# Loads as streams of their own, exchanges on two queues and a new order of requests in a gated mix of a long convolution and a dilated window attention

## The chip, the core and the metric

The kernel runs on one core of a Trainium2 chip. The core has five engines with instruction queues of their own: TensorE (PE, matrix products), VectorE (DVE), ScalarE (ACT), GpSimd (POOL) and SyncE (SP), which here does nothing but issue transfers. Transfers issued by SP go through the transfer queue that the profile calls q1, those of POOL through q0, and the few of ACT through q10; all three are served by the same 16 DMA engines of the core. The metric is device time in microseconds (us), lower is better. Three runs of the kernel before gave 229.2, 229.69 and 222.53 us, median 229.2.

## The reference, cut to what matters

```python
# x = A_q, k, v: [1, 2048, 640] bf16; shift_k: [640, 4]; ssm_k: [640, 2048]; ssm_D: [640]; wqkv: [640, 1920]; wo: [640, 640]
def A(q, k, v):                                   # H3-like branch
    k_shift = causal convolution of k over the sequence with 4 taps per channel (shift_k)
    kv = k_shift * v
    y = irfft(rfft(pad(kv)) * rfft(pad(ssm_k)))[:2048]      # causal convolution of length 2048, per channel
    return q * (y + kv * ssm_D)
def B(x):                                         # attention branch, 32 heads of 20 features
    q, k, v = split(x @ wqkv)
    logits = q[s] . k[s - 2w] for w = 0..7, times 20 ** -0.5, masked below 0
    return softmax(logits) @ v[s - 2w], heads joined, @ wo
g = sigmoid((x * gate_w).sum(-1))
out = g * A(x, k, v) + (1 - g) * B(x)
```

## The kernel before, in words

**Attention.** The rows of x are loaded into `xn` in eight pieces of 256 rows, transposed on PE (L445) into `xT`, even and odd positions apart, so that the dilation of two becomes a plain window. v is projected in 36 units of five matmuls (L521), and the gate in 20 (L534). q and k are projected (L568) for five feature tiles of 128 features (`ft` 0 to 4); one tile needs 12 units of five matmuls, six for q and then six for k (in the first tile they alternate). A unit's result is copied to a staging tile `stg`. Since a head has 20 features and the scores need every head at a partition that is a multiple of 32, the rows of each head are moved from `stg` by transfers of up to 20 rows, the **exchanges** (L618, `fragger`), into three sets of tiles `kb`, `qb`, which in the orders below carry the numbers 80/81, 82/83 and 84/85. A set holds four heads, one **head group**; the eight groups take the three sets in turn. For each group PE computes scores in five score groups (L642), ACT exponentiates each in two halves (L650, `ETall<-PS`), PE multiplies with v (L674) and DVE normalises (L684, L686).

**Convolution.** The four taps run on DVE in eight chunks (L467 to L482), the product with v behind them (L486). The long convolution is a transform in two steps: step one (L705 for the filter h, L701 for the signal u), step two (L724, with the table G), each for two halves P = 0, 1 of the channels; results are copied out of PSUM by ACT (L243) or DVE (L245). For the filter a copy `Hw` with swapped partitions is made by the **swaps** (L820): per half four pairs of transfers of 320 KB each, and from the second pair of a half on a one-column copy on POOL (L814) makes each pair wait until the pair before has landed. The **products** of the two spectra (L756) run on DVE, in 11 steps per half with two instructions each; the first needs the half's whole `Hw`. Then follow the inverse step one (L835), and the last step (L912), whose output `yb` is multiplied by the gated q (L890 scales q by g, L924 multiplies), added to the attention result `bl` (L926) and stored (L929). The output projection of the attention branch (L869) fills PE in between; its result is scaled into `bl` by ACT (L874) or DVE (L876).

**What sets the order.** Every part is a Python generator that yields requests (`Req`): which engine it wants, what it depends on, how many of four PSUM slots it takes. A string of some 1,100 letters, `ORDER`, says which stream is served next, and a `-` ahead of a letter gives the request to the second of two engines that it allows (ACT or DVE for a copy). The instructions of each engine stand in the order in which the requests were served, and each engine runs its own in that order. A request that waits therefore holds up everything behind it on its engine; on SP this is every later load and exchange. In the kernel before, the first loads are written out in `heads()`, in a fixed order; all later loads hang on the exchanges, through `bulk(ft)`, which `fragger` runs after the exchanges of a feature tile. Seven of the exchanges (q of the first feature tile) are issued by SP, the other 65 by POOL. `paced` loads have a small POOL memset ahead of the transfer.

## Time and profile before

| | us |
|---|---|
| three runs | 229.2, 229.69, 222.53 |
| median of them | 229.2 |
| profiled execution, its own time | 224.23 |
| its span | 222.5 |
| busy in the span: PE, DVE, ACT, POOL | 204.3, 185.0, 174.9, 51.1 |

The span is the time from the first to the last event that the profile shows; the profiled execution took 1.7 us more than its span. Three of the five engines are busy for 79% to 92% of the span, so no engine alone sets the time, and the busy figure of PE counts matmuls whose ends are modelled. The page is therefore read by stages: a table of windows gives each engine's busy time within a stretch, the chain of waits says what ended last at each place, the timelines give the start of single instructions, and the groups by line and shape the mean duration of one. In a timeline the second number is how long a piece lasted; instructions of one engine overlap a little, so the distance of two starts is less than the duration.

### The profile page before, as it was taken

How to read it: one execution, taken by the hardware profiler on the slowest of the kernel's cores; microseconds unless marked ns; L12 is line 12 of the kernel's file. 1: busy time of each engine (PE TensorE's matmuls, PEld its weight loads, DVE VectorE, ACT ScalarE, POOL GpSimd, SP SyncE). 2: the span in 40 equal slices, each digit the busy share in tenths (PEclk: the TensorE clock that was granted, in tenths of full speed). 3: DMA queues.
4: the chain of work that ended last, by engine and by line, in shares of the span. 5: the costliest groups of instructions: out<-in, count | busy, mean ns of one | idle time of the engine just before them, and what ended most of it. 6: DMA issues, size and time to landing. Idle time of an engine off the chain costs nothing.

```text
span 222.5 us, 8401 instructions
## 1 busy us (share of the span) xinstructions
PE 204.3 (92%) x3577; PEld 165.8 (75%) x3577; DVE 185.0 (83%) x261; ACT 174.9 (79%) x253; POOL 51.1 (23%) x129
## 2 busy tenths in 40 slices
PE   7999999999999999699997867999999999979990
PEld 3777987696777577466685756889888899979880
DVE  4745778997998898569898978998999997859992
ACT  0264487769998898599999988998999999478770
POOL 7980711470617044402450000000000000000000
PEclk9999999999999999999999699999999999999999
DMA  6999789599999999803993396678567082003645
GB/s 199 349 237 275 188 180 205 133 168 149 208 182 197 163 151 155 140 4 52 183 171 74 85 214 152 172 174 213 122 142 227 4 184 55 3 3 91 152 106 136
DMA packets 69049, 33.35 MB, mean 150 GB/s; under 512 B 51476, under 2 KB 66708, under 8 KB 69012
## 3 DMA queue, kind: packets, MB, share of 16 engines
q1 hardware_dynamic: 65684, 27.66, 61.3%
q0 software_dynamic: 2880, 4.90, 9.9%
q8 instruction: 28, 0.46, 1.0%
q10 hardware_dynamic: 448, 0.26, 0.4%
q14 instruction: 9, 0.07, 0.1%
HBM read 19.51 MB, written 2.62 MB: 100 GB/s over the span
## 4 chain that ended last, share of the span: by engine, by line
PE 51%; DVE 20%; ACT 10%; DMA 8%; issue 7%; POOL 2%; DVEq 0%; POOLq 0%; ACTq 0%
PE PS L568 14%; PE PS L521 8%; ACT ETall L650 6%; PE PS L835 6%; DMA kb<-stg 6%; DVE UC L245 5%; PE PS L869 4%; PE PS L724 4%; PE PS L674 3%; DVE SX L245 3%; PE PS L642 3%; DVE q L926 2%; DVE yb L245 2%; ACT H L243 2%; DVE q L924 2%
## 5 line engine op out<-in xcount | busy, mean ns | idle before, releaser
L650 ACT ACTIVATE ETall<-PS 121x912 bf16<-121x912 f32 (+1 forms) x80 | 63.8, 864 | 8.1 <-PE PS L642 7.7
L568 PE MATMUL PS<-xT,Wqk 128*128 128x342 bf16 (+1 forms) x300 | 49.7, 310 | 0.6 <-ACT stg L243 0.3
L243 ACT CAST UC<-PS 128x1024 bf16<-128x1024 f32 (+2 forms) x49 | 44.4, 1030 | 4.0 <-DVE UC L245 3.1
L568 PEld LDWEIGHTS <-Wqk 128*128 128x128 bf16 x300 | 27.4, 97 | 14.3 <-issue 0.5
L521 PE MATMUL PS<-WvT,xT 128*121 128x320 bf16 x180 | 27.5, 300 | 0.1
L467 DVE TENSOR_TENSOR KX<-KX 128x1280 bf16<-128x1280 bf16 x32 | 25.3, 820 | 0.3
L618 POOL DMA_DIRECT2D qb<-stg x29 | 14.6, 506 | 45.8 <-ACT stg L243 30.5
L869 PE MATMUL PS<-wo,oT 128*128 128x320 bf16 x160 | 24.4, 302 | 0.1
L521 PEld LDWEIGHTS <-xT 128*121 128x121 bf16 x180 | 23.4, 134 | 1.4
L243 ACT CAST stg<-PS 128x363 bf16<-128x363 f32 (+1 forms) x39 | 17.1, 471 | 7.8 <-PE PS L568 7.5
L869 PEld LDWEIGHTS <-oT 128*128 128x128 bf16 x160 | 21.1, 145 | 1.5 <-issue 0.5
L724 PEld LDWEIGHTS <-G 64*128 64x128 bf16 x512 | 18.2, 93 | 4.9 <-issue 3.7
L618 POOL DMA_DIRECT2D kb<-stg x36 | 18.1, 511 | 15.8 <-ACT stg L243 7.6
L642 PE MATMUL PS<-qb,kb 31*128 31x114 bf16 x576 | 16.0, 212 | 5.1 <-DMA kb<-stg 2.3
L245 DVE CAST stg<-PS 128x342 bf16<-128x342 f32 (+1 forms) x21 | 11.0, 522 | 11.7 <-PE PS L568 9.4
L642 PEld LDWEIGHTS <-kb 31*128 31x128 bf16 x576 | 9.4, 93 | 13.5 <-issue 9.8
L674 PEld LDWEIGHTS <-ETall 121*128 121x128 bf16 x576 | 17.4, 96 | 2.1 <-issue 0.5
L674 PE MATMUL PS<-VW,ETall 121*128 121x63 bf16 (+2 forms) x576 | 18.2, 184 | 0.6 <-DVE SX L245 0.3
L835 PE MATMUL PS<-F,Hw 128*128 128x128 bf16 x160 | 18.1, 219 | 0.0
L874 ACT ACTIVATE bl<-PS,omg 128x320 bf16<-128x320 f32 x31 | 16.1, 566 | 2.4 <-PE PS L869 1.9
L835 PEld LDWEIGHTS <-Hw 128*128 128x128 bf16 x160 | 17.9, 114 | 0.0
L245 DVE CAST UC<-PS 128x1024 bf16<-128x1024 f32 x13 | 15.3, 1219 | 2.6 <-ACT UC L243 1.2
(75 smaller groups left out, 334.1 us busy)
## 6 DMA issues: line engine op xcount, KB each, us to landing
xn<-in_A_q_dram SPq DMA_DIRECT2D x8, 320.0 KB
h_lin<-in_A_ssm_k_dram SPq DMA_DIRECT2D x16, 160.0 KB
vin<-in_A_v_dram SPq DMA_DIRECT2D x8, 320.0 KB
Hw<-H SPq DMA_DIRECT2D x8, 320.0 KB
q<-in_A_q_dram SPq DMA_DIRECT2D x8, 320.0 KB
Hw<-SX SPq DMA_DIRECT2D x8, 320.0 KB
kb<-stg POOLq DMA_DIRECT2D x28, 85.1 KB, 5.5
out_dram<-q SPq DMA_DIRECT2D x16, 120.0 KB
```

The costliest lines, as they stand in the source:

```text
L243: nc.scalar.copy(dst, src)
L245: nc.vector.tensor_copy(dst, src)
L467: eng.tensor_tensor(d, kin[:, n + 3 - j:n + 3 - j + m, :], w.to_broadcast([128, m, QC]), ALU.mult)
L521: nc.tensor.matmul(ps[0:BK, 0:320], lhsT=xT[:, dt, s0:s0 + BK], rhs=Wv[:, dt, 320 * hp:320 * hp + 320], start=(dt == 0), stop=(dt == NDT - 1))
L568: nc.tensor.matmul(ps[:, 0:n], lhsT=Wqk[:, dt, w, 128 * ft:128 * ft + 128], rhs=xT[:, dt, s0:s0 + n], start=(dt == 0), stop=(dt == NDT - 1))
L618: (nc.sync if near else nc.gpsimd).dma_start(dst[r0:r0 + rows, 0:wd], stg[fa - f0:fb - f0, 0:wd])
L642: nc.tensor.matmul(psum(g, h4 // 2)[:, h4 % 2, BQ * bb:BQ * bb + BQ], lhsT=kb[r:r + DH + NF, BK * b:BK * b + 128], rhs=qb[r:r + DH + NF, B ...
L650: nc.scalar.activation(ETall[0:BK, e, :, 0:BQ * nb], psum(g, k)[0:BK, :, 0:BQ * nb], ACT.Exp, scale=SCALE)
L674: nc.tensor.matmul(O[:, (b - b0) // 6, c0:c0 + 21 * nh], lhsT=ETall[0:BK, e, hh, BQ * bb:BQ * bb + 128], rhs=VW[0:BK, b, 4 * t + h4:4 * t ...
L724: nc.tensor.matmul(ps[:, c, 160 * jj:160 * jj + 160], lhsT=G[rows, j0 + jj, 64 - 64 * rr:192 - 64 * rr], rhs=Am[rows, rr].rearrange("p o ( ...
L835: nc.tensor.matmul(d, lhsT=st[(key, P)][:, c, o + il // 4, :, il % 4], rhs=M[:, k, :], start=(k == 0), stop=(k == 1), skip_group_check=True)
L869: nc.tensor.matmul(op, lhsT=oT[:, ft].rearrange("p h m a -> p a (h m)")[:, t, :], rhs=wo[:, ft, 320 * n:320 * n + 320], start=(ft == 0), s ...
```

## The change

- The loads of x, of the weights (`load_w0`, `load_w1`, `load_wv`), of k, of h, of the table G and of v become eight kinds of streams of their own, each with a letter in `ORDER`, and are no longer tied to the exchanges of a feature tile. k is loaded in six pieces of rows and not three; the first four of them have no POOL memset ahead. The tap weights `wraw` are issued by ACT and not by SP.
- Every exchange but those of q in the first feature tile may go to POOL or SP, as `ORDER` says. 39 now stand on SP (7 before) and 33 on POOL (65 before).
- The products take six steps per half and not 11: five of two steps each (1,920 columns per instruction, 960 before) and a last one of 640 columns. Each half has 12 product instructions, and not 22.
- `ORDER` is new as a whole, and with it the order on every engine. The constants that changed beside it (`LAND`, `STARTS`, `PIPE0`, `us`, `move`, costs) are estimates for the tool that made `ORDER`; they put out no instruction.

```diff
-KROWS = [(42, 64), (20, 42), (0, 20)]
+KROWS = [(53, 64), (45, 53), (37, 45), (29, 37), (13, 29), (0, 13)]
+FIRST = 4
...
 ORDER = """
-a-aa-aw-wa-aw-ww-wiiai-iiaaiaa-aia-iii-aiaa-ii-iiii-ii-iiiicifffccccw-wwww-wwwwfwwwwf-wffffwwwwwwcwcccccwwwdw-wdwddddi-wfccccccii
+ap-apquppqpptaaa4-a6-66666iia-aia-aa-attt-iiitti-iraii-aaai-iri-iivfu-iitiiiiii5tcff6fi-cc-ccc66fffff6666c-cc6666666666-66-66666cc
...
+    def load_x():
+        for a in range(2, 8):
+            yield from load(f"x{a}", xn[:, a], raw(x2, 256 * a * D, [[2 * D, 128], [D, 2], [1, D]]), 1150.0)
+
+    def load_w0():
+        for w in range(2):
+            yield from load(f"W0{w}", Wqk[:, :, w, 0:128], W3[:, :, w, 0:128], 800.0)
...
-            yield from paced(f"k{k}{q}", kin[32 * q:32 * q + 32, 3 + n0:3 + n1, :], raw(k2, n0 * D + QC * q, [[64 * D, 32], [D, n1 - n0], [1, QC]]), 62.0 * (n1 - n0))
+            yield from (paced if k >= FIRST else load)(f"k{k}{q}", kin[32 * q:32 * q + 32, 3 + n0:3 + n1, :], raw(k2, n0 * D + QC * q, [[64 * D, 32], [D, n1 - n0], [1, QC]]), 48.0 * (n1 - n0))
...
-    def bulk(ft):
-        if ft == 0:
-            yield from load_k(1)
-            yield from load_k(2)
-            yield from load_corners()
-            yield from small()
-            yield from load_h(0)
-        if ft == 1:
-            for a in range(4):
-                yield from load_G(a)
-                yield from load_v(0, a)
...
+    def load_ks():
+        for k in range(len(KROWS)):
+            yield from load_k(k)
+        yield from load_corners()
+
+    def load_h0():
+        yield from small()
+        yield from load_h(0)
+
+    def load_Gs():
+        for a in range(4):
+            yield from load_G(a)
+
+    def load_vs(c):
+        for a in range(4):
+            yield from load_v(c, a)
+
+    def load_h1():
+        yield from load_h(1)
...
+        for q in range(4):
+            nc.scalar.dma_start(wraw[32 * q:32 * q + 32].rearrange("p c j -> p (c j)"), raw(A_shift_k, 4 * QC * q, [[0, 32], [1, 4 * QC]]))
...
-                    g = yield Req("G", 510.0, deps, move=28.0 * rows)
-                (nc.sync if near else nc.gpsimd).dma_start(dst[r0:r0 + rows, 0:wd], stg[fa - f0:fb - f0, 0:wd])
+                    g = yield Req("GS", dict(G=510.0, S=450.0), deps, move=28.0 * rows)
+                (nc.sync if g.eng == "S" else nc.gpsimd).dma_start(dst[r0:r0 + rows, 0:wd], stg[fa - f0:fb - f0, 0:wd])
...
-            yield from bulk(ft)
...
+    PG = [(0, 2), (2, 4), (4, 6), (6, 8), (8, 10), (10, 11)]
...
     def products(P):
-        for k, (j0, n) in enumerate(JS):
+        for k0, k1 in PG:
+            j0 = JS[k0][0]
+            n = sum(JS[k][1] for k in range(k0, k1))
             for key in "hw":
-                r = yield Req("D", 68.0 + 0.521 * 320 * n, [ev(f"todo{P}{k}"), ev(f"hw{P}")])
+                r = yield Req("D", 68.0 + 0.521 * 320 * n, [ev(f"todo{P}{k}") for k in range(k0, k1)] + [ev(f"hw{P}")])
...
-                u_slot, swaps, load_T, load_wo, op_tr, outproj, final):
+                u_slot, swaps, load_x, load_w0, load_w1, load_wv, load_ks, load_h0, load_Gs, load_h1, load_T, load_wo, op_tr, outproj, final):
         plan.add(gen(), gen.__name__)
-    for gen in (load_q, vproj, h_stream, u_stream, products, inverse1):
+    for gen in (load_q, load_vs, vproj, h_stream, u_stream, products, inverse1):
```

**The exchange of the fifth head group.** Before, POOL issues the exchanges of the fourth feature tile one behind the other, q's (`qb`) first and then k's (`kb`); `kb_82<-stg 16x2178` is the last that the fifth group needs. POOL before:

```order
L328 MEMSET vin 32x1 x4
L618 DMA qb_83<-stg 16x2052
L618 DMA qb_85<-stg 20x2052 x4
L618 DMA qb_81<-stg 20x2052
L618 DMA qb_81<-stg 12x2052
L618 DMA kb_82<-stg 16x2178
L618 DMA kb_84<-stg 20x2178 x4
```

In the changed kernel the same transfer stands on SP, with loads of k (`KX`), of the table G and of v (`vin`) around it. SP after:

```order
L623 DMA qb_83<-stg 16x2052
L324 DMA KX<-in_A_k_dram 32x13x160
L324 DMA G<-cf_G 128x3x512
L623 DMA qb_85<-stg 20x2052
L324 DMA KX<-in_A_k_dram 32x13x160
L623 DMA qb_85<-stg 20x2052
L623 DMA qb_81<-stg 12x2052
L623 DMA kb_82<-stg 16x2178
L623 DMA kb_84<-stg 20x2178 x2
L324 DMA KX<-in_A_k_dram 16x3x160
L324 DMA vin<-in_A_v_dram 32x64x80 x2
```

The exchange moved from POOL's queue to SP's, where it waits for the copy into `stg` with three later loads right behind it.

**The swaps.** `Hw<-H` are the eight transfers of the first half, `Hw<-SX` those of the second, `q` the rows of x for the last step, `wo` the output weights, `SX<-cf_T` the table of the last step. SP before:

```order
L820 DMA Hw<-H_294 64x5x512 x2
L886 DMA q_2391<-in_A_q_dram 32x8x640
L820 DMA Hw<-H_294 64x5x512 x2
L886 DMA q_2391<-in_A_q_dram 32x8x640
L820 DMA Hw<-H_294 64x5x512 x2
L886 DMA q_2391<-in_A_q_dram 32x8x640
L820 DMA Hw<-H_294 64x5x512 x2
L820 DMA Hw<-SX 64x5x512 x2
L323 DMA wo<-in_B_wo_dram 128x5x640
L820 DMA Hw<-SX 64x5x512 x6
L323 DMA SX<-cf_T 128x4x512 x2
```

SP after:

```order
L548 DMA g_nat<-WvT 32x1x16 x4
L324 DMA G<-cf_G 128x3x512
L324 DMA wo<-in_B_wo_dram 128x5x640
L893 DMA q_2498<-in_A_q_dram 32x8x640 x4
L827 DMA Hw<-H_292 64x5x512 x8
L827 DMA Hw<-SX 64x5x512 x4
L324 DMA SX<-cf_T 128x4x512
L827 DMA Hw<-SX 64x5x512 x4
L324 DMA SX<-cf_T 128x4x512
L893 DMA q_3409<-in_A_q_dram 32x8x640 x4
```

The loads of q and `wo` moved ahead of the swaps, and the first half of the T table in between. What the swaps of the first half read also comes later: on PE the last matmuls of step two for H (L724, L728 after) stood ahead of the scores of the seventh head group, and stand now between the third and the fourth score group of the eighth.

**The last stage on DVE.** Before, scalings of q (`TENSOR_SCALAR q`) stand between the copies of the last step's output (`CAST yb`) and its use. DVE before:

```order
L245 CAST UC<-PS 128x128x8 x5
L890 TENSOR_SCALAR q_2391<-q_2391,g_nat 128x640 x2
L245 CAST yb_3616<-PS 128x2x3x160
L924 TENSOR_TENSOR q_2391<-yb_3616,q_2391 128x1920
L890 TENSOR_SCALAR q_3452<-q_3452,g_nat 128x640 x2
L926 TENSOR_TENSOR q_2391<-q_2391,bl 128x1920
L890 TENSOR_SCALAR q_3452<-q_3452,g_nat 128x640
L245 CAST yb_3616<-PS 128x2x3x160
```

DVE after:

```order
L246 CAST UC<-PS 128x128x8
L897 TENSOR_SCALAR q_3409<-q_3409,g_nat 128x640 x8
L246 CAST UC<-PS 128x128x8 x4
L246 CAST yb_3629<-PS 128x2x3x160
L897 TENSOR_SCALAR q_2498<-q_2498,g_nat 128x640
L931 TENSOR_TENSOR q_2498<-yb_3629,q_2498 128x1920
L933 TENSOR_TENSOR q_2498<-q_2498,bl 128x1920
L883 TENSOR_SCALAR bl<-PS,omg 128x320
```

All scalings of q but one moved ahead of the first `yb`. Over the whole last stage DVE has two `yb` copies and not five, one scaling of q and not eight, and three results of the output projection and not one; PE has 15 units of the output projection there (21 before), since six moved into the stage before.

62 lines of the change are left out of this document (23 added, 39 removed).

## The prediction

> **What bounds the kernel now.** First comes the page's own span, then the same execution by stages: each engine's busy time in five stretches that I cut at events. They are cut at the first scores, at the exponentials of the fifth head group (93.9), at the first copy of the transformed signal u (143.8) and at the start of the last step (196.2).
>
> ```profile
> span 222.5 us, 8401 instructions
> ```
> ```profile
> 0.00:30.00 30.00, 28.39 (x226) 22.20 (x226) 19.10 (x31) 11.08 (x18) 19.33 (x45) 1.00 0.95 243
> 30.00:93.90 63.90, 61.10 (x955) 44.58 (x954) 55.09 (x82) 52.70 (x88) 23.63 (x64) 1.00 1.04 170
> 93.90:143.80 49.90, 43.60 (x987) 33.46 (x986) 42.28 (x53) 46.88 (x63) 7.57 (x17) 0.97 0.61 124
> 143.80:196.20 52.40, 50.73 (x797) 47.31 (x797) 48.27 (x71) 48.36 (x61) 0.56 (x3) 1.00 0.49 120
> 196.20:222.50 26.30, 20.45 (x617) 18.26 (x616) 20.23 (x26) 15.88 (x27) 0.00 (x0) 0.99 0.41 103
> ```
>
> The columns after the length are PE, weight loads, DVE, ACT, POOL, granted clock, share of the DMA engines and GB/s. PE leads up to 93.9, ACT (94%) from there to 143.8; then PE, DVE and ACT are all above 92%; in the last stretch PE and DVE are level. A gain in one stage therefore counts only as far as the next engine lets it. Two rows of the chain of waits and the PE timeline show where PE waits for transfers:
>
> ```profile
> 67.99 6.96 DMA kb<-stg
> 74.99 0.38 PE PS L642 x13
> ...
> 87.27 0.51 POOL kb L618
> 87.78 5.66 DMA kb<-stg
> ```
> ```profile
> 63.95 0.91 PE L568 MATMUL PS<-xT,Wqk 128*128 128x349 bf16 x5
> ...
> 74.05 0.56 PE L642 MATMUL PS<-qb,kb 31*128 31x114 bf16 x3
> ...
> 81.29 0.36 PE L642 MATMUL PS<-qb,kb 31*128 31x114 bf16 x12
> 81.59 0.92 PE L568 MATMUL PS<-xT,Wqk 128*128 128x349 bf16 x5
> 82.34 1.45 PE L674 MATMUL PS<-VW,ETall 121*128 121x63 bf16 x48
> ...
> 85.43 0.92 PE L568 MATMUL PS<-xT,Wqk 128*128 128x349 bf16 x5
> 86.19 0.84 PE L521 MATMUL PS<-WvT,xT 128*121 128x320 bf16 x5
> ...
> 91.31 0.23 PE L642 MATMUL PS<-qb,kb 31*128 31x114 bf16 x3
> 93.46 0.38 PE L642 MATMUL PS<-qb,kb 31*128 31x114 bf16 x13 [1.92 <-DMA kb<-stg]
> ```
>
> The last projection for the fifth group ends at 86.19, its scores begin at 91.31 and stop until 93.46. For the fourth group the same distance is 64.7 to 74.05, and still the exchange comes 0.4 late.
>
> **The change part by part.** *Exchanges.* I call the PE work between the last projection of a feature tile and the first score that needs it the lead. For the fifth group it was 5.1 (86.19 to 91.31); in the new order one unit of L521 fewer stands ahead of it. For the fourth it was 9.3; now 24 score matmuls, 48 of L674 and 25 of L568 stand there, by the rows above 2 × 0.3 + 1.4 + 5 × 0.76 = 5.8. So the new order starts scores earlier and leaves exchanges about 5 us. Their price, from issue to landing, is in these answers (issue row, then landing):
>
> ```profile
> L618 POOL DMA_DIRECT2D qb<-stg x6: 501/504/521, 38.2 to 40.7; - x6
> DMA to landing us min/median/max: 3.4/3.8/4.1
> ...
> L618 POOL DMA_DIRECT2D kb<-stg x8: 499/501/516, 66.5 to 70.0; - x8
> DMA to landing us min/median/max: 4.7/7.0/8.2
> ...
> L618 SPq DMA_DIRECT2D qb<-stg x7: 667/725/939, 21.3 to 26.5; - x7
> ```
>
> 3.8 where little else moved, 7.0 at worst, both from POOL; landing from SP does not show. On SP the transfer stands behind whatever SP issued before. But SP stops at each exchange until `stg` is written, and meanwhile the loads ahead of it run out; so I take the row with little traffic, 3.8, between 3.4 and 8.2. For the fifth group: scores could start at 91.31 − 0.77 (one L521 unit) − 0.38 (the fourth group's wait, if gone) = 90.2. The projection then ends at 85.4, the copy takes 0.6, SP's issue 0.7, landing 3.8: 90.5. I allow 0.1 for such waits in earlier groups. Scores go on at 90.6 and not at 93.46: **−2.9**, between −3.3 and +3.3 (second rival).
>
> *From there to the first copy of u.* ACT gets one `stg` copy, one copy of 1,024 and one of 960 columns more and one of 640 fewer. DVE gets seven more tap instructions (a chunk of the convolution) and two large copies fewer.
>
> ```profile
> L243 ACT CAST SX<-PS 128x1024 bf16<-128x1024 f32 x4 | 3.8, 1046 | 0.0
> ...
> L467 DVE TENSOR_TENSOR KX<-KX 128x1280 bf16<-128x1280 bf16 x32 | 25.3, 820 | 0.3
> ```
>
> ACT: about 1.5 copies of 1.05, **+1.5**; DVE: 7 × 0.8 − 2 × 1.2 = +3.2. ACT bounds this stretch with 3.0 idle; DVE has 7.6 idle that covers its 3.2. If cover and ACT's idle serve fully, the term is 0; if DVE's idle stays as it is, +3.1. First copy of u: 143.8 − 2.9 + 1.5 = 142.4.
>
> *Products over six steps.* 20 instructions fewer, but longer ones:
>
> ```profile
> 158.35 0.65 DVE L756 TENSOR_TENSOR H<-UC,H 128x960 bf16<-128x960 bf16 x1
> 158.91 0.65 DVE L756 TENSOR_TENSOR Hw<-UC,Hw 128x960 bf16<-128x960 bf16 x1
> ...
> 172.79 0.65 DVE L756 TENSOR_TENSOR SX<-UC,SX 128x960 bf16<-128x960 bf16 x1
> ...
> 185.97 0.22 PE L835 MATMUL PS<-F,SX 128*128 128x128 bf16 x1
> ```
> ```profile
> L869 PE MATMUL PS<-wo,oT 128*128 128x320 bf16 x105 | 15.6, 302 | 0.0
> ...
> L924 DVE TENSOR_TENSOR q<-yb,q 128x1920 bf16<-128x1920 bf16 x4 | 4.6, 1159 | 0.4
> ...
> L245 DVE CAST yb<-PS 128x960 bf16<-128x960 f32 x4 | 4.6, 1153 | 2.2 <-PE PS L912 2.2
> L890 DVE TENSOR_SCALAR q<-q,g_nat 128x640 bf16<-128x640 bf16 x8 | 2.8, 380 | 0.0
> ...
> L876 DVE TENSOR_SCALAR bl<-PS,omg 128x320 bf16<-128x320 f32 x1 | 0.5, 546 | 0.0
> ```
>
> (The second fence groups the last stretch alone.) Two old steps start 2 × 0.56 apart; one new one, by L924's 1,920 columns, lasts 1.16 and starts some 0.09 less after the one before, as the old ones do (0.65 against 0.56). Per replaced pair that is between +0.04 and −0.1, and with 20 pairs between +0.8 and −2; I take −1. Each step now waits for two copies of u, which DVE's other work there covers.
>
> *The middle and the last stretch.* Six units of L869 move from the last stretch into the middle: 30 × 15.6 / 105 = 4.5 of PE. DVE's middle also gets four copies of 960 (4 × 1.15) and seven scalings (7 × 0.38), less one copy to ACT (1.2) and 1 for the products: +5. Its middle has 4.1 idle, PE's 1.7. PE bounds: +4.5 if it has no slack, +2.8 if it uses all; I take **+4.3**. In the last stretch DVE loses three `yb` copies (3 × 1.15, the smallest is shorter: 3.1) and seven scalings (2.7) and gets two `bl` (1.1): −4.7 in means, whose rows overlap a little, so −4.5. PE loses 4.5 as well; ACT, with three `yb` more and eight `bl` fewer, stays below both. DVE first, then PE: **−4.2**, between −3.6 and −4.7.
>
> *Loads.* The order of the first loads changes little before 30: PE idles 1.6 there, ahead of its first matmul; ±0.5, taken as 0. Later loads now stop behind waiting exchanges; who waits for that is the fourth rival.
>
> Sum: −2.9 + 1.5 + 4.3 − 4.2 = −1.3, so a span of 221.2. The profiled execution took 224.23, 1.7 above its span: **222.9 us**. Its ends come from the terms' ends without the rivals: −5.7 to +2.0 (the exchanges between −3.3 and −2.5), which gives 218.5 to 226.2. Two of the three runs shown lie at 229.2 and 229.7, 5 above the profiled one, and the third at 222.5; the sum stands on the lower level.
>
> **The rivals.**
>
> *The swaps come late (slower).* The copies after the swaps show a pair's period, and two PE rows the distance from the eighth group's fourth score group to the first matmul on u:
>
> ```profile
> 149.83 0.19 POOL L814 COPY Hw<-Hw 128x1 bf16<-128x1 bf16 x1 [10.16 <-DMA Hw<-SX]
> 156.37 0.19 POOL L814 COPY Hw<-Hw 128x1 bf16<-128x1 bf16 x1 [6.35 <-DMA Hw<-SX]
> 161.83 0.19 POOL L814 COPY Hw<-Hw 128x1 bf16<-128x1 bf16 x1 [5.27 <-DMA Hw<-SX]
> ```
> ```profile
> 136.65 0.34 PE L642 MATMUL PS<-qb,kb 31*128 31x114 bf16 x12 [0.23 <-ACT ETall L650]
> ...
> 143.03 10.32 PE L701 MATMUL PS<-F,vin 128*128 128x256 bf16 x80
> ```
>
> A pair takes c = 5.5 alone and 6.5 with `wo` beside it. H is now finished just ahead of that score group: 142.4 − 0.8 − 6.4 ≈ 135. Three periods to the fourth issue, then 1.3 of issuing, the next half's first pair landing c + 1 later, three more: the second half's `Hw` is there at 137.3 + 7c, so at 175.8 or 182.8. DVE wants it 29.0 after the first copy of u as before (143.8 to 172.79), and 5 later for its new work: 176.4. PE's inverse step on the second half (row 185.97) came 42.9 after 143.03, which is now 141.6, and has 4.5 more ahead: it starts at 189.0. DVE's products of that half take 11.5 (ten old steps at 2 × 0.56, a smaller one, less half of the 1) and are over at 187.9. From 177.5 on, c = 5.7, the swaps set the end. At 6.5 they cost 182.8 + 11.5 − 189.0 = 5.3: 228.2 us. For it: the start is later by 15. Against: `wo` and q now run ahead of the swaps.
>
> *Exchanges land from SP no sooner than from POOL.* Copy 0.6, issue 0.7 and landing then exceed the lead: in the second group (lead five units of L521, one of L568, 12 score matmuls: 4.9) by 1.1 at 4.7, in the fourth by 2.5 at 7.0, in the fifth (lead 4.3) by 2.7 at 5.7. Its exponentials come 3.3 later than before and not 2.9 earlier: 222.9 + 6.2 = 229.1 us; at half of that, 226. For it: the DMA share of 1.04 up to 93.9. Against: 3.8 at 38 to 41. The Trainium skill, "DMA: Bandwidth & Descriptors", section "Issuing engines are not separate DMA queues", states that transfers of any issuing engine end on the same 16 DMA engines and interleave, and that another issuer saves only its own issue time. By that rule alone it is this rival, 229.1; the trace agrees as far as landing follows traffic (3.8 against 7.0 from one issuer).
>
> *ACT and DVE overlap better.* With the stretch to u at 0, the middle at +2.8 and the last at −4.7: 222.5 − 2.9 + 0 + 2.8 − 4.7 + 1.7 = 219.4 us. For it: DVE's idle 7.6. Against: no stretch has all three engines above 97%.
>
> *Loads starve behind exchanges.* 39 exchanges stop SP, and with it k and v. Taps or the product with v then come late by about one chunk, 7 × 0.8 = 5.6, half of it under DVE's idle: 225.7 us. Against: DVE's taps stand later in the new order, and no DVE row up to 144 names a load as what it waited for.
>
> **How the numbers follow.** Forecast 0.42, swaps 0.15, exchanges 0.20, overlap 0.13, loads 0.10. The range is 218 to 229.5: it takes in the ends of the forecast and the overlap below, and the swaps and most of the second rival above; what lies outside (swaps beyond 6.7 a pair, all groups late) I put at 0.15. About 2% is what a measurement of this kernel can tell from no change. Against the profiled 224.23 this is 219.7 to 228.7: the overlap case and the forecast's lower end are faster (0.16), the upper ends slower (0.22). Against the median 229.2 it is 224.6 to 233.8: most of the forecast is faster (0.56), little is slower (0.06). Weighing both alike: faster 0.36, slower 0.14, same 0.50.
>
> **What would show it.** Right: scores of the fifth group (L642) without a wait at about 90.6, first copy of u near 142.4, the last step starting near 199.2, 22 before the end. Wrong: waits of L642 for `kb<-stg` over 1 us (second rival); DVE products waiting for `Hw` (first); taps or L486 waiting for loads (fourth). An ACT that idles over 4 between the two marks, or a last stretch still above 25, would make the sum wrong.

## The result and the profile after

The kernel after took 231.4 us (median of six runs, 230.0 to 232.9) against 225.1 us (222.5 to 229.7) for the kernel before: a ratio of 1.033, with a 95% interval from 1.029 to 1.037. Some executions of a kernel are a per cent or more slower than its others; medians here take all executions and ratios leave the slow ones out, so a ratio is not the quotient of two medians. The kernel is slower, where 222.9 us had been forecast. Its profiled execution took 231.55 us, with a span of 229.6.

Cut at the same four events as before (first exponential of the fifth head group, first copy of u, first matmul of the last step, end), the windows of the kernel after read as follows; the columns after the length are PE, weight loads, DVE, ACT, POOL, granted clock, share of the DMA engines and GB/s.

```profile
30.00:96.45 66.45, 62.95 (x954) 45.18 (x953) 49.86 (x74) 51.52 (x85) 12.01 (x44) 0.97 0.75 138
96.45:148.96 52.51, 46.97 (x986) 35.80 (x985) 46.88 (x61) 48.28 (x66) 5.73 (x19) 0.90 0.77 146
148.96:206.62 57.66, 54.74 (x835) 51.43 (x833) 51.96 (x61) 50.67 (x65) 1.39 (x5) 1.00 0.51 121
206.62:229.64 23.02, 16.83 (x587) 14.27 (x586) 16.38 (x18) 13.69 (x22) 0.00 (x0) 1.00 0.46 118
```

The four stretches lasted 93.89, 49.89, 52.44 and 26.24 us before, and last 96.45, 52.51, 57.66 and 23.02 now: 2.6, 2.6 and 5.2 more, 3.2 less. (The four events are read to the hundredth here, which is why they differ by up to 0.1 from the cuts of the prediction.) Only the last change is a gain.

The first loss begins far ahead of the fifth group. The PE timeline of the kernel after, around the first scores of the second, the fourth and the fifth head group (L646):

```profile
47.85 0.84 PE L526 MATMUL PS<-WvT,xT 128*121 128x320 bf16 x5
48.62 0.40 PE L646 MATMUL PS<-qb,kb 31*128 31x114 bf16 x3
51.48 0.38 PE L646 MATMUL PS<-qb,kb 31*128 31x114 bf16 x13 [2.45 <-DMA kb<-stg]
...
75.67 0.38 PE L646 MATMUL PS<-qb,kb 31*128 31x114 bf16 x14 [0.41 <-DMA kb<-stg]
...
95.97 0.39 PE L646 MATMUL PS<-qb,kb 31*128 31x114 bf16 x16
```

The wait sits at the second group and not at the fifth, which starts without any, but late. The chain of waits names the transfer, and the instructions of the tile `kb` between 44 and 52 show who issued exchanges there and how long GpSimd's took to land:

```profile
45.92 5.50 DMA kb<-stg
```
```profile
L623 POOL DMA_DIRECT2D kb<-stg x5: 501/501/510, 45.4 to 47.5; - x5
L623 SPq DMA_DIRECT2D kb<-stg x2: 725/734/742, 45.1 to 45.9; - x2
...
DMA to landing us min/median/max: 2.6/5.2/5.5
```

Two exchanges of the second feature tile's k rows went out on SyncE at 45.1 and 45.9. They are the ones that the second group needs. GpSimd sent five others, rows for the two groups after it, from 45.4 on. The second of SyncE's took 5.50 us.

### The profile page after: what moved, and what is told of

It reads as the page before. It is cut to its first block, busy times and chain, and to the rows that moved or that the text cites. A ratio compares the mean times of both kernels' runs of the same rounds, so it can differ in the third digit from the quotient of the medians.

```text
span 229.6 us, 8417 instructions
## 1 busy us (share of the span) xinstructions
PE 208.6 (91%) x3577; PEld 167.9 (73%) x3577; DVE 183.6 (80%) x240; ACT 175.4 (76%) x254; POOL 35.4 (15%) x97
## 4 chain that ended last, share of the span: by engine, by line
PE 60%; DVE 18%; DMA 9%; ACT 5%; issue 4%; SPq 2%; DVEq 0%; ACTq 0%
PE PS L573 16%; PE PS L876 10%; PE PS L526 7%; PE PS L678 6%; DMA kb<-stg 6%; PE PS L728 5%; PE PS L842 5%; DVE UC L246 4%; PE PS L646 4%; ACT ETall L654 3%; PE PS L919 2%; DMA xn<-in_A_q_dram 2%; DVE SX L246 2%; PE PS L450 2%; DVE oT L246 2%
## 5 line engine op out<-in xcount | busy, mean ns | idle before, releaser
L573 PE MATMUL PS<-xT,Wqk 128*128 128x342 bf16 (+1 forms) x300 | 50.1, 313 | 0.4 <-ACT stg L244 0.3
L244 ACT CAST UC<-PS 128x1024 bf16<-128x1024 f32 (+2 forms) x45 | 41.4, 1005 | 6.5 <-PE PS L842 3.4
L244 ACT CAST stg<-PS 128x342 bf16<-128x342 f32 (+1 forms) x41 | 18.2, 470 | 12.1 <-PE PS L573 10.9
L728 PEld LDWEIGHTS <-G 64*128 64x128 bf16 x512 | 19.4, 97 | 5.3 <-issue 4.2
L646 PE MATMUL PS<-qb,kb 31*128 31x114 bf16 x576 | 17.9, 219 | 4.6 <-DMA kb<-stg 2.9
L246 DVE CAST UC<-PS 128x1024 bf16<-128x1024 f32 (+1 forms) x17 | 19.8, 1204 | 1.6 <-PE PS L842 1.3
L646 PEld LDWEIGHTS <-kb 31*128 31x128 bf16 x576 | 10.2, 96 | 14.5 <-issue 9.5
L678 PEld LDWEIGHTS <-ETall 121*128 121x128 bf16 x576 | 18.7, 100 | 1.7 <-issue 0.2
L678 PE MATMUL PS<-VW,ETall 121*128 121x63 bf16 (+2 forms) x576 | 19.6, 190 | 0.0
L246 DVE CAST stg<-PS 128x363 bf16<-128x363 f32 (+1 forms) x19 | 9.9, 523 | 7.2 <-PE PS L573 5.4
L881 ACT ACTIVATE bl<-PS,omg 128x320 bf16<-128x320 f32 x29 | 14.6, 541 | 1.0 <-PE PS L876 0.4
L244 ACT CAST VW<-PS 121x320 bf16<-121x320 f32 x21 | 9.1, 431 | 8.0 <-PE PS L526 8.0
L690 DVE TENSOR_TENSOR VW<-PS,rd 114x960 bf16<-114x960 f32 (+1 forms) x16 | 14.5, 908 | 0.6
```

The costliest lines, as they stand in the source:

```text
L244: nc.scalar.copy(dst, src)
L246: nc.vector.tensor_copy(dst, src)
L573: nc.tensor.matmul(ps[:, 0:n], lhsT=Wqk[:, dt, w, 128 * ft:128 * ft + 128], rhs=xT[:, dt, s0:s0 + n], start=(dt == 0), stop=(dt == NDT - 1))
L646: nc.tensor.matmul(psum(g, h4 // 2)[:, h4 % 2, BQ * bb:BQ * bb + BQ], lhsT=kb[r:r + DH + NF, BK * b:BK * b + 128], rhs=qb[r:r + DH + NF, B ...
L678: nc.tensor.matmul(O[:, (b - b0) // 6, c0:c0 + 21 * nh], lhsT=ETall[0:BK, e, hh, BQ * bb:BQ * bb + 128], rhs=VW[0:BK, b, 4 * t + h4:4 * t ...
L728: nc.tensor.matmul(ps[:, c, 160 * jj:160 * jj + 160], lhsT=G[rows, j0 + jj, 64 - 64 * rr:192 - 64 * rr], rhs=Am[rows, rr].rearrange("p o ( ...
```

## The experiments

The table gives every run with a profile that is read here: its median, its ratio to the kernel before with the 95% interval, and the length of the four stretches in its profiled execution, which can lie a per cent beside the median. The runs were spread over several chips and each ratio is to the kernel before on the run's own chip, so between two runs the ratios are the safer comparison.

| kernel | median us | ratio to before | to 5th group | to u | middle | last |
|---|---|---|---|---|---|---|
| before | 225.1 | | 93.89 | 49.89 | 52.44 | 26.24 |
| after | 231.4 | 1.033 (1.029 to 1.037) | 96.45 | 52.51 | 57.66 | 23.02 |
| all_pool | 226.3 | 1.004 (0.999 to 1.009) | 92.14 | 51.43 | 57.26 | 23.02 |
| need_first | 228.0 | 1.013 (1.005 to 1.022) | 93.95 | 51.03 | 57.87 | 23.59 |
| two_on_sp | 229.6 | 1.023 (1.013 to 1.034) | 97.28 | 51.70 | 57.32 | 23.18 |
| all_sp | 236.0 | 1.047 (1.037 to 1.056) | 95.88 | 53.65 | 59.73 | 23.69 |
| t1_lead | 229.1 | 1.019 (1.011 to 1.027) | 94.97 | 51.89 | 57.51 | 22.88 |
| clock_fill | 232.1 | 1.033 (1.020 to 1.046) | 95.15 | 52.84 | 57.65 | 23.11 |
| old_front | 228.8 | 1.016 (1.006 to 1.026) | 93.29 | 53.23 | 55.95 | 22.92 |
| old_back | 242.1 | 1.077 (1.063 to 1.092) | 95.54 | 50.99 | 66.12 | 25.72 |
| before_six | 224.5 | 0.995 (0.990 to 0.999) | 93.53 | 50.37 | 52.40 | 26.46 |
| late_v | 223.3 | 0.993 (0.988 to 0.997) | 92.39 | 49.89 | 52.43 | 26.41 |
| pool_eleven | 232.6 | 1.033 (1.020 to 1.046) | 92.24 | 50.84 | 65.53 | 23.22 |
| eleven_no_link | 225.0 | 1.001 (0.996 to 1.007) | 91.90 | 51.58 | 55.92 | 24.06 |
| pool_swaps | 236.8 | 1.052 (1.044 to 1.060) | 91.11 | 53.82 | 66.32 | 24.59 |

**All exchanges on GpSimd.** The mark ahead of the letter `c` in the table of requests picks SyncE; it is taken out everywhere (one line of the nine, with its old line ends).

```diff
-cctiddi-7idieddidtfffuiedtidcdd-iidt4dtedf-iidftte4ii-idtttif-iid4ddeidufuuuuittdfe-cfucc-c-cc-cc-ciii-ci-c-idcddiifffiid-cdcci-ie
+cctiddi-7idieddidtfffuiedtidcdd-iidt4dtedf-iidftte4ii-idtttif-iid4ddeidufuuuuittdfecfucccccccciiicic-idcddiifffiidcdcci-ie
```

> The kernel after with every exchange issued by GpSimd; the order of all other requests is kept. Theory (short leads: an exchange takes 4.5 to 5.5 us to land from either queue, so the scores of the second head group wait at 51.5 whoever issues it): 229 to 233 us, with a wait of 2 to 4 us ahead of the second group's scores. Rival (the SP queue delays exchanges behind its loads and its limit of transfers under way): the wait falls below 1 us and the time to 225 to 228 us.

226.3 us: 5 us less than the kernel after, level with the kernel before. My theory at that point (short leads, any queue) was wrong, and the rival's times came: it is the queue. The rival's reason is another matter. No run here shows a limit of transfers under way, and in two_on_sp below the exchange was just as late although SyncE had issued no load for 8.5 us. The same view of `kb` and the PE timeline, of this run:

```profile
L623 POOL DMA_DIRECT2D kb<-stg x7: 498/498/525, 45.7 to 48.8; - x7
...
DMA to landing us min/median/max: 2.3/2.9/5.7
```
```profile
48.99 0.38 PE L646 MATMUL PS<-qb,kb 31*128 31x114 bf16 x16
```

The seven exchanges are the same ones, now in one queue, so that the second group's two are first, and the first landings take 2.3 us. The second group's scores start at 48.99 and go on without a wait; in the kernel after they started at 48.62 and then stopped for 2.45 us. The fifth group's exponentials come 1.8 us earlier than before, where 2.9 had been forecast.

**A longer lead for the second group.** Three projection units move from behind its first scores to ahead of them; on VectorE two of their copies move with them.

```
 L246 CAST stg<-PS 128x342
 L246 CAST VW<-PS 121x16x20
+L246 CAST stg<-PS 128x342
+L246 CAST VW<-PS 121x16x20
 L688 RECIPROCAL rd_88<-PS 114x24
 L690 TENSOR_TENSOR VW<-PS,rd_88 114x6x80
-L246 CAST stg<-PS 128x342
-L246 CAST VW<-PS 121x16x20
```

> The kernel after with three projection units (two of the values, one of queries and keys, 2.2 us of TensorE work) moved from behind the first scores of the second head group to ahead of them. Theory (the lead is too short, and the idle TensorE that follows also brings a stretch of half clock at 52 to 56): the wait of 2.45 us falls to under 0.5, the half-clock stretch near 52 goes, and the time falls by 2.5 to 4.5 us, to 227 to 229 us. Rival (later stages are bound by ScalarE and VectorE, and give the gain back): 230.5 to 232 us.

```profile
51.60 0.38 PE L646 MATMUL PS<-qb,kb 31*128 31x114 bf16 x13 [0.56 <-DMA kb<-stg]
```

229.1 us, just outside of the theory's 227 to 229, and the wait is 0.56. The exchange comes when it came, but TensorE has done 2.2 us of other work meanwhile, and the fifth group follows 1.5 earlier. So a longer lead hides the late transfer; it does not make it early.

**The front of before with the rest of after, and the reverse.** The table of one kernel up to the first request on u, then the rest of the other's; the k pieces and the product steps follow their half.

> All requests up to the first on the transformed u in the order, on the queues and in the pieces of the kernel before; from there on the order and the six-step products of the kernel after. Theory (the first copy of u came 5.2 us later in the kernel after, and the rest takes 1.9 us longer): first copy of u at 143.5 to 144.5 and a time of 225 to 227 us. Rival (the longer rest comes from swaps that start late, and these start early here): the rest takes no longer than before, or gains the 2 to 3 us of the forecast: 220 to 224.5 us.

> All requests up to the first on the transformed u as in the kernel after; from there on the order of the kernel before, with products in eleven steps. Theory (losses add): first copy of u at 148.5 to 149.5, the rest 78 to 80 us, 227.5 to 230.5 us in all. Rival (the rest is held by the swaps, which this order begins after the first work on u): 231 to 235 us.

Both missed. With the old front the rest took 78.9 us (55.95 and 22.92), as long as before (78.7), so the rival was right on it: with swaps that start early the new rest costs nothing. But TensorE stood still twice ahead of u in that run, for 2.2 us in all, and no releaser shows:

```profile
137.68 1.23 PE L678 MATMUL PS<-VW,ETall 121*128 121x42 bf16 x40 [0.95 <-issue]
...
144.69 1.15 PE L728 MATMUL PS<-SX,G 64*128 64x160 bf16 x28 [1.24 <-issue]
```

Its cause stays open. The reverse came to 242 us. The wait is that of the second half's products for `Hw`, and GpSimd's one-element copy that links two swap pairs lasted 6.39 us where it usually lasts 0.19:

```profile
188.25 0.66 DVE L763 TENSOR_TENSOR SX<-UC,SX 128x960 bf16<-128x960 bf16 x1 [11.74 <-DMA Hw<-SX]
```
```profile
170.16 6.39 POOL L821 COPY Hw<-Hw 128x1 bf16<-128x1 bf16 x1 [5.25 <-DMA Hw<-SX]
```

**Two exchanges to GpSimd, two back to SyncE.** If sharing between queues is the cause, the second group's two exchanges alone must show it, in both directions. The first run is the kernel after with these two on GpSimd, ahead of the others; the second is all_pool with them on SyncE.

The rows of GpSimd in need_first (against after), then those of SyncE in two_on_sp (against all_pool):

```
 L623 DMA qb_85<-stg 20x2052
+L623 DMA kb_82<-stg 12x2178
+L623 DMA kb_82<-stg 20x2178
 L623 DMA kb_84<-stg 20x2178 x4
```
```
 L324 DMA KX<-in_A_k_dram 32x8x160
+L623 DMA kb_82<-stg 12x2178
+L623 DMA kb_82<-stg 20x2178
 L324 DMA wgz<-in_gate_w_dram 128x5x1
```

> The kernel after with two of its exchanges moved from SyncE to GpSimd: the first two of the k rows of the second feature tile, which the second head group needs, so that GpSimd now issues them ahead of the third group's exchanges. Everything else as after. Theory A (two queues share the transfer engines, so the second group's rows travel interleaved with rows that nobody needs yet; one queue keeps them in order of need): the wait of 2.45 us falls below 0.7, scores of the second group go on at 49 to 50 instead of 51.5, and the time falls by 2.4 to 4 us, to 227 to 229 us. Theory B (SyncE's stops and the loads that it then issues in a burst slow whatever travels): the wait stays above 1.5 us, 230 to 232 us.

> The run with all exchanges on GpSimd, and only two of them back on SyncE: the first two of the k rows of the second feature tile (the reverse of the step before). Theory A (rows on a second queue share the transfer engines with the others): they take 4.5 to 5.5 us to land instead of 2.4, the second group's scores wait 1.5 to 2.5 us, and the time is 228 to 230 us instead of 226.3. If the order of need does not matter: no wait and 225.5 to 227 us.

The PE timeline of need_first with the landings of `kb` there, then the PE timeline and the chain of waits of two_on_sp:

```profile
49.91 0.22 PE L646 MATMUL PS<-qb,kb 31*128 31x114 bf16 x1 [0.45 <-DMA kb<-stg]
50.37 0.38 PE L646 MATMUL PS<-qb,kb 31*128 31x114 bf16 x13 [0.23 <-DMA kb<-stg]
```
```profile
DMA to landing us min/median/max: 3.8/4.4/5.9
```
```profile
50.89 0.56 PE L646 MATMUL PS<-qb,kb 31*128 31x114 bf16 x13 [2.39 <-DMA kb<-stg]
```
```profile
45.39 5.46 DMA kb<-stg
```

SyncE's issues in two_on_sp (the last load before the two exchanges, and what follows them), and what each queue took of the 16 engines' time between 45.39 and 50.85:

```profile
35.44 0.52 SPq L324 DMA_DIRECT2D KX<-in_A_k_dram  x1
44.51 1.65 SPq L623 DMA_DIRECT2D kb<-stg  x2
46.20 0.65 SPq L324 DMA_DIRECT2D wgz<-in_gate_w_dram  x1
```
```profile
q0 software_dynamic: 252, 0.48, 42.0%
q1 hardware_dynamic: 1248, 0.30, 35.1%
```

Two of the 72 exchanges are worth 3.4 us one way (231.4 to 228.0) and 3.3 the other (226.3 to 229.6), of the 5.1 that lie between after and all_pool; by the ratios it is close to 0.02 each way, of 0.029. In two_on_sp only these two exchanges of that part are on SyncE, nothing stood ahead of them in its queue, and the landing is 5.46 us again. GpSimd's queue (q0) took the larger share of the engines' time meanwhile. The share of q1 holds the two exchanges and also the loads that SyncE issued right behind them, so it is not shown that GpSimd's five are all that they compete with. need_first tells how much of it the order is: there the same loads travel on SyncE, the needed rows are first in GpSimd's queue, and the second of them lands in 3.8 us, against 2.3 in all_pool, where no load travels beside it, and 5.5 with the order lost. What is left in need_first are waits of the first group (0.83 at 31.5), of the second (0.45 and 0.23) and of the fourth (0.76 at 73.2).

**All exchanges on SyncE.** Here every `c` that may choose has the mark.

> The kernel after with every exchange issued by SyncE; the order of all requests is kept. Theory A (one queue keeps the order of need, whichever it is): the second group's scores wait less than 0.7 us and the time is 226 to 229 us, near the run with all exchanges on GpSimd. Theory B (exchanges from SyncE are slow, or loads stand behind them too long): waits of 2 us or more for exchanges or loads, and 231 us or more.

The second group's scores start at 49.94 without a wait, as the theory of one queue says, and still the time is 236 us. The waits moved to what stands behind the exchanges in SyncE's queue, and to what they hold:

```profile
45.73 2.88 PE L526 MATMUL PS<-WvT,xT 128*121 128x320 bf16 x20 [1.14 <-DMA WvT<-in_B_wqkv_dram]
```
```profile
71.50 0.79 ACT L244 CAST stg<-PS 128x342 bf16<-128x342 f32 x2 [3.58 <-DMA qb<-stg]
```

The weights of the second half come 1.14 late, and ScalarE waits 3.58 for a `stg` that an exchange still holds. So the order of need within one queue is right for scores, and a queue shared with the loads held up both. Why the middle stretch of this run is longer too (59.73) is open.

**The half clock behind the wait.** In the kernel after, a stretch of half clock follows the idle 2.45 us. Fifteen matmuls of no use fill that time in the next run; they go into a free bank and are never read.

```diff
+    def fill():
+        g = yield Req("P", 0.0, xdeps(0, HS) + [ev("Wv0")], take=1)
+        ps = psum(g)
+        for n in range(15):
+            nc.tensor.matmul(ps[0:BK, 0, 0:320], lhsT=xT[:, n % NDT, X0:X0 + BK], rhs=Wv[:, n % NDT, 0:320], start=True, stop=True, skip_group_check=True)
+        yield Req("P", 0.0, [g.done], give=g.banks)
```

> The kernel after with fifteen matmuls of no use (2.3 us, into a free bank, never read) ahead of the first scores of the second head group, so that TensorE has hardly an idle stretch there although the exchange comes as late as before. Theory (of the loss behind the wait, 1.4 us is a stretch of half clock that idleness brings): scores of the second group go on at 51.5 to 52 as before, clock 1.00 from 50 to 60 instead of 0.83, scores of the third group at 61 to 62 instead of 63.0, 0.8 to 2 us less in all (229.5 to 230.7 us). Rival (the half clock costs nothing there, ScalarE or VectorE set the pace): third group at 63, 231 to 232 us.

First the kernel after from the first exponential of the second group to that of the third, the slow part alone, and three later stretches; then clock_fill from exponential to exponential, and the same later ones:

```profile
51.91:63.45 11.54, 11.24 (x185) 7.92 (x185) 6.59 (x11) 9.38 (x14) 1.02 (x2) 0.85 0.85 134
...
52.20:55.60 3.40, 3.40 (x49) 2.50 (x48) 1.46 (x3) 2.50 (x4) 0.00 (x0) 0.51 1.16 165
...
120.00:130.00 10.00, 8.43 (x162) 5.74 (x158) 8.39 (x9) 8.24 (x12) 0.00 (x0) 0.66 0.58 89
130.00:140.00 10.00, 7.11 (x188) 5.58 (x184) 9.11 (x10) 9.79 (x12) 0.00 (x0) 1.00 0.75 206
140.00:150.00 10.00, 9.94 (x218) 9.03 (x213) 8.56 (x13) 8.58 (x12) 0.20 (x1) 0.83 0.71 143
```
```profile
51.86:62.09 10.23, 9.96 (x185) 7.18 (x186) 6.65 (x11) 9.27 (x14) 1.05 (x3) 1.00 0.96 151
...
120.00:130.00 10.00, 7.32 (x164) 4.61 (x159) 8.86 (x10) 8.79 (x12) 0.00 (x0) 0.83 0.50 100
130.00:140.00 10.00, 8.46 (x181) 7.04 (x181) 8.59 (x13) 8.90 (x11) 0.00 (x0) 0.75 0.76 189
140.00:150.00 10.00, 9.58 (x199) 8.78 (x197) 8.15 (x10) 8.66 (x12) 0.19 (x1) 0.91 0.70 146
```

At that place the theory holds: the same 185 matmuls take 10.23 us at full clock and 11.54 with the half-clock stretch, so it costs 1.3. In the whole it does not show by the medians (232.1 against 231.4, intervals overlapping), although the profiled execution of clock_fill ended 0.9 earlier (spans 228.8 and 229.6). What the clock does later does not explain it: both kernels meet half clock again between 120 and 150, at other places but the same in sum (0.66, 1.00 and 0.83 against 0.83, 0.75 and 0.91).

**Swaps ahead of wo and q.** To all_pool's order: H's last units of the second step, the last quarter of G and the first half's swaps earlier.

> The kernel after with all exchanges on GpSimd, and with the last three units of the second step on H, the load of the table's last quarter and the first half's eight swaps moved ahead, the swaps also ahead of the loads of wo and of the first q. Theory (the products of the second half wait 1.4 us for a late Hw, and the middle stretch is 1 to 2 us longer for it): first swap pair landed near 135 instead of 142.4, no wait of the products for Hw, 1 to 2.5 us less than the 226.3 of the run with all exchanges on GpSimd: 224 to 225.5 us. Rival (TensorE and ScalarE bound the middle, the swaps only fill it; or the moved transfers collide): 226 to 228 us.

The first pair did land at 137.3 and the products did not wait for `Hw`, but the time is 236.8: q now stands behind the swaps, and VectorE stops at its scaling. Its waits between 143 and 178, and the chain:

```profile
DVE q L897 <- DMA q<-in_A_q_dram: 8.5, 1, 8.5
```
```profile
153.44 10.49 DMA q<-in_A_q_dram
```

So this does not price late swaps; the next runs do.

**Products: six steps alone, and eleven steps in the new order.** before_six is the kernel before with the new grouping; pool_eleven is all_pool with the old one.

```diff
-    PG = [(0, 2), (2, 4), (4, 6), (6, 8), (8, 10), (10, 11)]
+    PG = [(k, k + 1) for k in range(11)]
```

> The kernel before with its products in six steps instead of eleven; all else as before. Forecast of the step: 1 us less (0.8 more to 2 less), 223 to 226 us against 225. Rival (longer instructions make the products and what follows wait for two copies of u each): 0.5 to 2 us more, 225.5 to 227 us.

> The run with all exchanges on GpSimd, with products in eleven steps as in the kernel before. Theory (a step over two pieces of u waits for the later one: 1.5 us of VectorE's idle time in the middle): that wait shrinks below 0.6 and the time is 0.5 less to 0.5 more (the ten extra fixed costs of about 0.05 us each per half): 225.8 to 226.8 us. If the six steps were worth the 1 us of the forecast in this order too: 227 to 227.8 us.

In the old order six steps gave 224.5 us, between 0.2 and 2.2 us less than before. The middle stretch shows none of it (52.40 against 52.44), although VectorE was busy 1.3 less there (46.98 against 48.27). In the new order eleven steps cost 6 us, beyond either expectation. The linking copies and the products of pool_eleven show how:

```profile
L821 POOL COPY Hw<-Hw x6: 186/190/3555, 142.0 to 172.7; 128x1 bf16<-128x1 bf16 x6
```
```profile
167.08 0.39 POOL L821 COPY Hw<-Hw 128x1 bf16<-128x1 bf16 x1 [5.48 <-DMA Hw<-SX]
172.68 3.56 POOL L821 COPY Hw<-Hw 128x1 bf16<-128x1 bf16 x1 [5.21 <-DMA Hw<-SX]
...
175.70 0.48 DVE L763 TENSOR_TENSOR Hw<-UC,Hw 128x640 bf16<-128x640 bf16 x1
183.59 0.66 DVE L763 TENSOR_TENSOR SX<-UC,SX 128x960 bf16<-128x960 bf16 x1 [7.41 <-issue]
```

The last copy begins at 172.7 and lasts 3.56 us, to 176.2: the moment at which VectorE's run of products ends (175.70 + 0.48). The last swap pair is issued only then, and the second half's products wait 7.41 us for it.

**Without the linking copies.** Each swap is issued as soon as its source is there.

```diff
-                    if last is not None:
-                        x = yield Req("G", 150.0, [last.done])
-                        nc.gpsimd.tensor_copy(Hw[:, c, o, 0, 0:1], Hw[:, lc, lo, 0, 0:1])
-                        d = [x.done]
-                    else:
-                        d = []
+                    d = []
```

> The run with all exchanges on GpSimd and products in eleven steps, without GpSimd's one-element copies between the swap pairs: each swap is issued as soon as its source is there. Theory (the last of these copies lasted 3.56 us because VectorE's products ran without a gap, and the last swap pair and the second half's products waited for it): the products of the second half wait under 2 us instead of 7.4, and the time falls from 232.6 to 226 to 229 us. Rival (the swaps themselves are too late, or swaps side by side hold up other transfers): 230 us or more.

> The run with all exchanges on GpSimd (six-step products), without GpSimd's one-element copies between the swap pairs. Theory (the products' wait of 1.4 us for the second half's Hw is the swaps' lateness, and unlinked swaps end earlier): that wait goes, 0.5 to 2 us less than 226.3. Rival (unlinked swaps crowd the engines, and instruction loads or wo come late): 226.5 to 230 us.

eleven_no_link: 225.0 us, 7.6 less than with the copies. The products run on from one half to the other without a gap (176.09, then 176.49), and the middle stretch is 55.92:

```profile
176.09 0.48 DVE L763 TENSOR_TENSOR Hw<-UC,Hw 128x640 bf16<-128x640 bf16 x1
176.49 0.65 DVE L763 TENSOR_TENSOR SX<-UC,SX 128x960 bf16<-128x960 bf16 x1
```

pool_no_link: 224.4 us, ratio 0.998 (0.992 to 1.004). That is 1.9 less than all_pool by the medians, as the theory says, but all_pool's interval (0.999 to 1.009) overlaps, so the gain is not shown. No profile of it is read here, so whether the wait for `Hw` went is not known either.

**Landing follows traffic, used.** late_v is before_six with two of the eight loads of v held back until the exchange that the fifth group waits for has been issued.

```
 L623 DMA kb_82<-stg 4x2178
-L329 MEMSET vin 32x1 x4
+L329 MEMSET vin 32x1 x2
 L623 DMA qb_83<-stg 16x2052
...
 L623 DMA kb_82<-stg 16x2178
+L329 MEMSET vin 32x1 x2
 L623 DMA kb_84<-stg 20x2178 x4
```

> The kernel before with products in six steps, and the last two of its loads of v moved behind the first k exchange of the fourth feature tile, which the fifth head group waits for. Theory (landing follows what else travels on the engines): that exchange lands in 3 to 4.5 us instead of 5.7, the fifth group's wait of 1.55 to 1.9 us falls below 0.7, and ScalarE, which bounds what follows, passes it on: 1 to 2 us less than the 224.5 of six steps alone: 222.5 to 223.5 us. Rival (the exchange is slow by itself or the gain is given back before the end): 224 to 225 us.

```profile
91.59 0.75 PE L646 MATMUL PS<-qb,kb 31*128 31x114 bf16 x16
```

The exchange that the group needs last, of late_v and then of before_six, from issue to landing:

```profile
kb<-stg POOLq DMA_DIRECT2D x1, 68.1 KB, 4.4
```
```profile
kb<-stg POOLq DMA_DIRECT2D x1, 68.1 KB, 5.8
```

SyncE's queue took 0.40 of the engines' time until this landing, and 0.61 in before_six. With less traffic beside it the exchange lands 1.4 us sooner, the fifth group's wait (1.55 in before_six) is gone, and its exponentials come 1.1 us earlier. The time is 223.3 us, 0.7% below the kernel before (interval 0.3% to 1.2%) and 8 us below the kernel after, the lowest median of the runs here. That the 1.1 us reach the end is not shown: the intervals of late_v and of before_six (0.990 to 0.999) overlap.

## Why the prediction was wrong

**The exchanges: the step that failed.** −2.9 was forecast, +2.6 came. The step reads: "SP stops at each exchange until `stg` is written, and meanwhile the loads ahead of it run out; so I take the row with little traffic, 3.8", and, for what comes before the fifth group, "I allow 0.1 for such waits in earlier groups". I counted loads as the traffic and overlooked the other exchanges. They are issued in the same burst on the other queue; the transfer took 5.50 us, and the second group, not the fifth, stopped for 2.45. Up to the fifth group the split over two queues costs 4.3 us (96.45 against 92.14 in all_pool); the stop, the half clock behind it (1.3) and the fourth group's 0.41 make about 4.2 of it. In the whole time the second group's two transfers alone are 3.3 to 3.4 us (need_first and two_on_sp). With all exchanges on GpSimd the term is −1.8, so the direction of the forecast was right for the order, and wrong for the split over two queues; the 1.1 us between −1.8 and −2.9 stay open.

Two readings under the 3.8 were off as well. The row is quieter, not quiet: the share of the DMA engines was 0.75 between 38.2 and 42, against 1.15 between 67 and 76, where an exchange took 7.0. And the views count a landing from the start of the issue, so the 0.7 for the issue stood in the sum twice; this erred to the slow side.

The second rival (exchanges land from SyncE no sooner, 229.1 us) named the side and the landing as the cause; it had 0.20. Its places were not right: it expected waits of 1.1, 2.5 and 2.7 us in the second, fourth and fifth group; they were 2.45, 0.41 and none. The second group's wait made everything later, and the later exchanges were nearly or quite in time. Its fifth group was 0.7 us too late, and the other stretches came 3.0 us longer than the forecast that it kept for them, which makes the 2.3 us beyond its figure.

The same transfer took 5.50 us in the kernel after and 2.3 in all_pool. The Trainium skill, "DMA: Bandwidth & Descriptors", section "Queues, rings and completion order", states that each DMA engine takes turns between the queues for which it has work, packet by packet. These runs agree: in all_pool, on one queue, the seven exchanges landed with the needed two first (2.4 and 2.3 us after their issue, the last 5.7), while in the kernel after the 32 rows of SyncE's two exchanges went out between 46.8 and 50.1 in turn with GpSimd's 96 rows, which went out between 46.4 and 51.5.

**From the fifth group to u.** +1.5 forecast, +2.6 measured; all_pool has 51.43 − 49.89 = +1.5. The size was right for the work. In the kernel after this stretch was granted 0.90 of the clock, before 0.97. The runs that have the order of the kernel after up to u line up by the clock of this stretch: 50.8 to 51.4 us at 0.97 (pool_eleven, old_back, need_first, all_pool), 51.6 to 51.9 at 0.93 (eleven_no_link, two_on_sp, t1_lead), 52.5 and 52.8 at 0.90 (after, clock_fill); only all_sp, whose exchanges stand behind loads, falls out of it (53.65 at 0.94). So the missing 1.1 us goes with the half clock; which of the two brings the other was not tested.

**Middle.** +4.3 forecast between 2.8 and 4.5, +5.2 measured. Two runs in which the swaps end early have 55.95 (old_front) and 55.92 (eleven_no_link), +3.5. So the work moved there was sized within its bounds, and 1.7 us is the first rival's mechanism in small: swaps are late, and VectorE stops for them. The kernel after's DVE timeline at the change of halves:

```profile
179.94 1.16 DVE L763 TENSOR_TENSOR H<-UC,H 128x1920 bf16<-128x1920 bf16 x1 [1.53 <-ACT UC L244]
...
184.80 1.16 DVE L763 TENSOR_TENSOR SX<-UC,SX 128x1920 bf16<-128x1920 bf16 x1 [1.83 <-issue]
```

The second wait is for `Hw` (in two_on_sp the same wait, of 1.48, is put down to `DMA Hw<-SX`): it is gone where swaps end early. The first is a step of two pieces of u that waits for the later one. The words of the prediction, "which DVE's other work there covers", did not hold for it, but no price shows: old_front has this wait (1.53) and a middle of 55.95, eleven_no_link does not have it and has 55.92. The rival's date was 137.3 + 7c for the second half's `Hw`, its price 5.3; the price was a third of that.

**Products.** −1 forecast, −0.7 measured in before_six by the medians (−2.2 to −0.2), with nothing to be seen in the middle; near in size, and where it comes from is not shown.

**Last stretch.** −4.2 forecast, −3.2 measured, outside its bounds. The rows gave VectorE 4.5 less; its busy time fell by 3.85 (20.23 to 16.38), and its idle time there grew from 6.1 to 6.6. The term was mis-sized because I subtracted means of groups, whose instructions overlap more than I allowed, and let no wait grow: VectorE now waits 1.0 us there for the projection's matmuls ahead of its scalings of `bl`, which it did not before.

**Loads.** The start was off by 0.4 (first scores at 30.60 after 30.20 before), within ±0.5. The fourth rival (loads starve behind exchanges) did not occur in the kernel after; all_sp shows that it exists.

In sum, −2.9, +1.5, +4.3 (the products' −1 among it) and −4.2 made the −1.3 of the forecast; +2.6, +2.6, +5.2 and −3.2 make the +7.2 that came.

## What to carry to other kernels

Here small transfers with a date did best in one queue, in the order in which they are needed, and apart from the bulk loads: the packets of the second queue shared the engines with those of the first, and what was needed first came later. Before a transfer's landing time is taken from a quiet row, list everything that the new order issues in the same few microseconds, on any queue. And when a run of work is moved, look for the small links on other engines that used to lie outside of it: here a one-element copy between two transfers.

## What was unexpected of the hardware

GpSimd's one-element copy takes 0.19 us, also beside VectorE's copies out of PSUM. Beside VectorE's products it took 3.56 us (pool_eleven) and 6.39 us (old_back), each time to the end of VectorE's run of products (176.2, and 176.01 + 0.49 in old_back against 170.16 + 6.39). The Trainium skill, "SBUF — State Buffer", section "Who interferes with whom", states that a VectorE instruction with two SBUF inputs contends with a GpSimd instruction that reads SBUF, and that the one that comes second is blocked. The runs agree on both kinds of instruction. They show one thing more: beside products that follow each other without a gap the copy can be kept out for the rest of the run, and not only for one instruction of 0.65 us. It need not be: an earlier copy beside the same run of products in pool_eleven took 0.39 us (at 167.08). In the runs with six-step products the longest of these copies took 0.64 us (after) and 1.16 us (clock_fill). What decides it stays open.

An idle 2.45 us of TensorE was followed by 3.4 us at half clock, and keeping TensorE busy with useless matmuls there avoided it, for 1.3 us at that place; that anything of it is left in the end is not shown.
